# Weight conversions queued behind the last norm's scaling on VectorE and the last high part on ScalarE

## The chip, the cores and the metric

The kernel runs on one core of a Trainium2 chip. The metric is device time in microseconds (us), from one launch. Before the change three runs took 999.49, 1002.72 and 1003.02 us; the median is 1002.72. Profiles come from one more execution.

## The reference

Three stages, one behind the other, in float32 (weights are given as float64 and are read as pairs of 32-bit words):

```python
# attention: batch 4, heads 8, 512 local + 32 global positions, head size 64
s_ll = where(|i - j| <= 32, scale * q_l @ k_l.T, -1e9);  s_lg = scale * q_l @ k_g.T
out_l = softmax([s_lg, s_ll]) @ [v_g, v_l];  out_g = softmax(scale * q_g @ [k_g, k_l].T) @ [v_g, v_l]
x = concat([out_g, out_l]) as 2176 tokens x 512
# first feed-forward, 512 -> 1536 -> 512
xn = x / sqrt(mean(x * x) + 1e-6) * rms_g
x = (silu(xn @ w_gate) * (xn @ w_val)) @ w_out
# second feed-forward, 512 -> 2048 -> 512, with a rational function of h
h = x @ w_in;  g = P(h) / (Q(h) + 1e-6);  out = g @ w_out
```

## The kernel before

**Numbers in two parts.** Each matmul operand is split into a high part (rounded, `xt[:, 0]`, `ah`, `w[:, 0]`) and a low part (what the rounding left, `xt[:, 1]`, `al`, `w[:, 1]`); three products stand for one. On TensorE lines 644, 645 and 648 are the three for gate (psg) and value (psv), lines 676 to 678 the three for the way down (psA).

**Blocks, units, groups.** The 2176 tokens are eight blocks of 288 or 256 tokens (two per batch, the numbers in names: xt_4 belongs to block 4, psA_5_0 to block 5, quarter 0). The 1536 columns of the first feed-forward are three groups of four weight tiles. Group 0 runs over all eight blocks, then group 1, then group 2. One call of `unit()` is one step of a generator: a half of the gate and value products of one weight tile, or a quarter of the way down of the block before.

**Norm.** Before a block's first product its x is normed (`norm_stages`): ScalarE squares, VectorE or GpSimd adds, TensorE sums over partitions (psN, line 590), VectorE adds the epsilon (line 595), ScalarE takes an exponential as first guess of the root (line 598), VectorE improves it in two rounds of three small steps on 128x3 (lines 601 to 603, tile sm), TensorE spreads sm over partitions (psR, line 608), VectorE scales x in four instructions (line 614). Then `chunk` splits x: the high part on ScalarE (line 633, xt), the low part on VectorE or GpSimd (line 635). After a unit `act` makes a from psg and psv: ScalarE tanh (line 660), VectorE lines 662 and 663, ScalarE the high part ah (line 665), VectorE or GpSimd the low part al (line 667).

**Weight conversions.** `Weights.stages` turns one raw tile of float64 words into a high and a low part: ScalarE lines 89 and 92, VectorE lines 98, 100, 104 and 108 (tile cv), ScalarE line 118 (the high part), VectorE line 121 (the low part). `Weights.step` goes on with the tiles in work by one stage; the main loop calls it once per unit from unit 72 on (line 1039). Names raw_g, raw_v, raw_o, raw_h and raw_p are raw tiles of w_gate, w_val, w_out, w_in and the second w_out; w_g_4747 and w_v_4768 are the first two converted tiles of group 1.

**What sets the order.** Attention, all eight norms and the first 58 units are written out token by token in `SCRIPT`; inside `manual_schedule` every engine takes them in that order. What is traced behind it is placed by the framework's scheduler, which orders instructions by dependences, priority and its own estimate of time, and may put later traced instructions of an engine between those of the script. `tc.issue_after(ins)` adds an edge without a semaphore: whatever the block traces on the engine of `ins` is put behind `ins` in that engine's queue. Each engine runs its queue in order. With line 1002 the eight PSUM banks of attention are given back; the first tile of the new pools (psA of block 5) waits until all readers of the old banks are done, among them the scaling that reads the last psR.

Of the kernel before, what the change touches and what calls it, by code (L numbers as in the profile page):

```python
# [14 lines left out]
AF = mybir.ActivationFunctionType  # L15
# [19 lines left out]
def _ap(t, dims, offset=0):  # L35
    return bass.AP(tensor=t.tensor, offset=t.offset + offset, ap=[list(t.ap[0])] + [list(d) for d in dims])
# [496 lines left out]
class FFN1:  # L533
# [40 lines left out]
    def norm_stages(self, blk):  # L574

        nc = self.nc
        nb = self.width(blk)
        t = lambda i: self.pool.tile([128, NB1], F32, tag=f"st{i}", name=f"st{i}_{blk}", bufs=1)[:, :nb]
        m, r, u = t(0), t(1), t(2)
        nc.scalar.activation(out=m, in_=self.xs(blk, 0), func=AF.Square)  # L580
        yield
        for c, q in ((1, r), (2, u), (3, r)):
            nc.scalar.activation(out=q, in_=self.xs(blk, c), func=AF.Square)
            yield
            self.pick().tensor_tensor(out=m, in0=m, in1=q, op=ALU.add)
            yield c == 3
        cols = [min(128 * j, nb - 128) for j in range((nb + 127) // 128)]
        ps = self.bank(self.acc, f"psN{blk}")
        for j, c0 in enumerate(cols):
            nc.tensor.matmul(ps[:, j : j + 1], m[:, c0 : c0 + 128], self.ones, start=True, stop=True)  # L590
        yield
        n = len(cols)
        sm = self.pool.tile([128, 3, 3], F32, tag="sm", name=f"sm{blk}", bufs=2)
        m, r, u = (sm[:, i, :n] for i in range(3))
        nc.vector.tensor_scalar(out=m, in0=ps[:, :n], scalar1=1e-6, scalar2=None, op0=ALU.add)
        yield
        r0 = ps[:, 4 : 4 + n]
        nc.scalar.activation(out=r0, in_=m.bitcast(I32), func=AF.Exp, scale=-self.LN2H / 2**23, bias=self.eps)
        yield 1
        for up, to in ((1.0 + 1.65e-4, r0), (1.0, r)):  # L600
            nc.vector.scalar_tensor_tensor(out=u, in0=r0, scalar=-0.5 * up, in1=m, op0=ALU.mult, op1=ALU.mult)
            nc.vector.tensor_tensor(out=u, in0=u, in1=r0, op=ALU.mult)
            nc.vector.scalar_tensor_tensor(out=to, in0=u, scalar=1.5 * up, in1=r0, op0=ALU.add, op1=ALU.mult)
            yield
        ps = self.bank(self.acc, f"psR{blk}")
        for j, c0 in enumerate(cols):
            a = 128 * j - c0
            nc.tensor.matmul(
                ps[:, 128 * j : c0 + 128], _ap(r[:, j : j + 1], [[0, 128]]), self.ident[:, a:128], start=True, stop=True
            )  # L610
        yield
        for c in range(4):
            v = self.xs(blk, c)
            nc.vector.scalar_tensor_tensor(  # L614
                out=v, in0=v, scalar=self.gam[:, c : c + 1], in1=ps[:, :nb], op0=ALU.mult, op1=ALU.mult
            )
            yield
# [32 lines left out]
    def act(self, k, blk, pss, use_silu):  # L650
        nc = self.nc
        nb = self.width(blk)
        t = lambda tag, dt, bufs: self.pool.tile([128, NB1], dt, tag=tag, name=f"{tag}{blk}_{k}", bufs=bufs)[:, :nb]
        a, ah, al = t("a", F32, 2), t("ah", F32R, 6), t("al", F32R, 5)
        self.acts[blk, k] = ah, al
        g, v = pss[0][:, :nb], pss[1][:, :nb]
        if use_silu:
            self.last_silu = nc.scalar.activation(out=a, in_=g, func=AF.Silu)
        else:
            nc.scalar.activation(out=a, in_=g, func=AF.Tanh, scale=0.5)  # L660
            yield
            nc.vector.scalar_tensor_tensor(out=a, in0=a, scalar=1.0, in1=g, op0=ALU.add, op1=ALU.mult)
        nc.vector.scalar_tensor_tensor(out=a, in0=a, scalar=1.0 if use_silu else 0.5, in1=v, op0=ALU.mult, op1=ALU.mult)
        yield
        nc.scalar.activation(out=ah, in_=a, func=AF.Copy)
        yield
        self.pick().tensor_tensor(out=al, in0=a, in1=ah.bitcast(F32), op=ALU.subtract)

# [53 lines left out]
def ffn2(tc, pool, pp, y_all, coef, wts, out, side, opool):  # L722
# [19 lines left out]
    for bi, (s0, n) in enumerate(BLK2):  # L742
        yt = split_y(bi)
        ntt = n // 128
        acc = [pp.tile([128, 512], F32, tag="psB", name=f"psB{bi}_{m}", bufs=4) for m in range(ntt)]
        act, mid = {}, {}

        def up(k):
# [105 lines left out]
def kernel(  # L854
# [7 lines left out]
    nc = tc.nc  # L862
# [5 lines left out]
    wts = Weights(tc, vpool, wide)  # L868
# [12 lines left out]
    def cols(w, k):  # L881
        return w[:, 128 * k : 128 * k + 128].rearrange("(c p) f -> p c f", p=128)

    def rows(w, k):
        return w[128 * k : 128 * k + 128].rearrange("(c p) f -> p c f", p=128)

    def group_loads(grp, pool):
        for kk in range(4):
            k = 4 * grp + kk
            yield lambda k=k, kk=kk: wts.load(("g", k), pool, f"w{2 * kk}", cols(w_gate, k))  # L890
            yield lambda k=k, kk=kk: wts.load(("v", k), pool, f"w{2 * kk + 1}", cols(w_val, k))
        for kk in range(4):
            k = 4 * grp + kk
            yield lambda k=k, kk=kk: wts.load(("o", k), pool, f"w{8 + kk}", rows(w_out1, k))
# [3 lines left out]
    def load_2(k):  # L898
        (ph, th), (po, to) = slots2[2 * k], slots2[2 * k + 1]
        wts.load(("h", k), ph, th, cols(w_in2, k))  # L900
        wts.load(("p", k), po, to, rows(w_out2, k))

    NB = 2 * B
# [5 lines left out]
    def norm_step():  # L909
        if norms and not wts.on(norms[0]):  # L910
            norms.pop(0)

    def unit():
        done[0] += 1
        next(units, None)
# [12 lines left out]
    ffn = FFN1(tc, f1pool, x, y, gam, wts, ident)  # L928
# [69 lines left out]
        assert next(rest, 0) == 0  # L998
    att.eng = ffn.eng = wts.eng = None
    assert done[0] == IN_ATTN  # L1000
    manual.close()
    ps_scope.close()
    attn_scope.close()
# [15 lines left out]
    for n in range(IN_ATTN, 36 * NB):  # L1019
        blk, u = divmod(n, 12)  # L1020
        norm_step()
        if n == 12 * NB:
            silu[0] = True
        if blk == NB + 1 and u == 0:
            for f in group_loads(2, wa):
                f()
            for i in range(12):
                k = 10 + i // 2
                key, src = (("h", k), cols(w_in2, k)) if i % 2 == 0 else (("p", k), rows(w_out2, k))
                scratch[key] = (wa, f"w{i}", dram.tile([128, 2, 512], I32, name=f"scr{i}"))  # L1030
                wts.load(key, spare, f"s{i % 3}", src, scratch[key][2], True)
        if blk == 2 * NB + 1 and u == 0:
            for k in range(6):
                load_2(k)
        if blk > 2 * NB and blk % 2 == 0 and u == 6:
            load_2(6 + (blk - 2 * NB) // 2 - 1)
        unit()
        if n >= 72:
            wts.step(nc.vector, 2 if blk < NB + 1 else 1)
    for u in range(4):  # L1040
        unit()
    ps_scope.close()
# [50 lines left out]
```

## Time and profile before

| | |
|---|---|
| median of three runs | 1002.72 us |
| the profiled execution | 999.14 us |
| its span, first to last instruction | 997.4 us |
| TensorE busy | 944.8 us, 95% |
| VectorE busy | 784.7 us, 79% |
| ScalarE busy | 601.8 us, 60% |
| GpSimd busy | 311.5 us, 31% |
| mean granted TensorE clock | 0.980 of full speed |

The span is cut into three parts: attention with the first units up to about 250 us, the rest of the first feed-forward up to about 600 us, the second feed-forward behind it. In rows of a timeline the first number is the start, the second the length in us; "x4" are four instructions merged to one row; the bracket at the end gives how long the engine had been idle and whose end released it. Engines are PE (TensorE), DVE (VectorE), ACT (ScalarE), POOL (GpSimd), SP (SyncE).

### The profile page before, as it was taken

Reading aid. Unit: us, or ns where it says so; the run is one execution under the profiler, and the core shown is the slowest. Engines: PE = TensorE matmul, PEld = TensorE weight load, DVE = VectorE, ACT = ScalarE, POOL = GpSimd, SP = SyncE. Lnnn points to the kernel's source line nnn. Section 1 sums busy time; section 2 is a strip of 40 time slices with the busy share of each in tenths; the row PEclk is TensorE's granted clock in tenths of the full one; section 3 lists DMA queues with packets and bytes.
Section 4 is the critical chain, followed back from the end, with each engine's and each line's share of the span. In section 5 each row is a group of like instructions: output and inputs, shape, how many; then the busy total and the mean of one; then the engine's idle time right before and its main releaser. Section 6 shows DMA issues by size and latency. Waiting matters only on the chain.

```text
span 997.4 us, 21577 instructions
## 1 busy us (share of the span) xinstructions
PE 944.8 (95%) x8224; PEld 868.6 (87%) x8224; DVE 784.7 (79%) x1891; ACT 601.8 (60%) x1382; POOL 311.5 (31%) x406
## 2 busy tenths in 40 slices
PE   6677999997999999999999998999999999999997
PEld 4465898876999999999999997979899898898895
DVE  5787678768979987459954538998989989989897
ACT  6667657877658546337543335666667666666674
POOL 5444966632000000000000023543444435435443
PEclk9788999999899999999999999999999999999999
DMA  8887754327124055025011053000000000000000
GB/s 202 202 184 152 153 107 96 94 66 276 51 85 170 22 200 202 22 86 190 23 43 43 2 182 114 1 1 32 1 2 32 1 33 1 1 32 1 1 32 23
DMA packets 107576, 78.79 MB, mean 79 GB/s; under 512 B 72320, under 2 KB 95696, under 8 KB 107472
## 3 DMA queue, kind: packets, MB, share of 16 engines
q1 hardware_dynamic: 100672, 62.36, 22.2%
q0 software_dynamic: 5712, 14.79, 5.2%
q8 instruction: 65, 1.06, 0.5%
q10 hardware_dynamic: 1088, 0.26, 0.1%
q14 instruction: 39, 0.32, 0.1%
HBM read 62.64 MB, written 10.75 MB: 74 GB/s over the span
## 4 chain that ended last, share of the span: by engine, by line
PE 65%; DVE 16%; DMA 7%; ACT 4%; SPq 4%; issue 2%; POOL 2%; ACTq 0%; POOLq 0%; DVEq 0%
PE psg L644 4%; PE psA L676 4%; PE psA L678 4%; PE psA L677 4%; PE psv L644 4%; PE psg L648 4%; PE psg L645 4%; PE psv L648 4%; PE psv L645 4%; PE psH L755 4%; PE psH L756 4%; PE psH L757 4%; PE psB L790 4%; PE psB L791 4%; PE psB L792 4%; SPq L232 3%
## 5 line engine op out<-in xcount | busy, mean ns | idle before, releaser
L755 PE MATMUL psH<-yt,w_h 128*128 128x384 f32 (+1 forms) x384 | 126.0, 329 | 1.2 <-ACT yt L737 0.7
L756 PE MATMUL psH<-yt,w_h 128*128 128x384 f32 (+1 forms) x384 | 125.4, 327 | 0.0
L163 POOL TENSOR_SCALAR gh<-p 128x384 fp32r<-128x384 f32 (+1 forms) x96 | 59.0, 615 | 210.4 <-DVE p L779 181.6
L757 PE MATMUL psH<-yt,w_h 128*128 128x384 f32 (+1 forms) x384 | 123.5, 328 | 0.8 <-DVE yt L738 0.8
L644 PE MATMUL psg<-xt,w_g 128*128 128x288 f32 (+1 forms) x384 | 115.3, 302 | 0.7 <-ACT xt L633 0.6
L676 PE MATMUL psA<-ah,w_o 128*128 128x288 f32 (+1 forms) x384 | 111.8, 294 | 3.1 <-DVE x L614 2.0
L790 PE MATMUL psB<-w_p,gh 128*128 128x512 f32 x272 | 107.8, 396 | 5.1 <-POOL gh L163 5.1
L644 PE MATMUL psv<-xt,w_v 128*128 128x288 f32 (+1 forms) x384 | 111.3, 291 | 0.0
L645 PE MATMUL psg<-xt,w_g 128*128 128x288 f32 (+1 forms) x384 | 111.1, 290 | 0.0
L645 PE MATMUL psv<-xt,w_v 128*128 128x288 f32 (+1 forms) x384 | 110.9, 290 | 0.0
L678 PE MATMUL psA<-al,w_o 128*128 128x288 f32 (+1 forms) x384 | 110.0, 290 | 0.0
L677 PE MATMUL psA<-ah,w_o 128*128 128x288 f32 (+1 forms) x384 | 110.0, 290 | 0.0
L781 POOL TENSOR_TENSOR gl<-p,gh 128x384 fp32r<-128x384 f32 (+1 forms) x96 | 106.7, 1112 | 8.4 <-PE psB L792 0.4
L791 PE MATMUL psB<-w_p,gh 128*128 128x512 f32 x272 | 107.2, 394 | 0.0
L648 PE MATMUL psg<-xt,w_g 128*128 128x288 f32 (+1 forms) x384 | 105.3, 291 | 0.7 <-DVE xt L635 0.5
L648 PE MATMUL psv<-xt,w_v 128*128 128x288 f32 (+1 forms) x384 | 104.9, 290 | 0.0
L94 POOL TENSOR_SCALAR raw_h<-raw_h 128x512 int32<-128x512 uint32 x1 | 0.6, 644 | 332.5 <-DMA raw_h<-in_moe_w_in_dram 332.5
L775 ACT ACTIVATE r<-q,cq 128x384 f32<-128x384 f32 (+1 forms) x96 | 57.3, 597 | 60.4 <-DVE q L765 59.6
L765 DVE SCALAR_TENSOR_TENSOR q<-q,bv,t 128x384 f32<-128x384 f32 (+1 forms) x96 | 68.5, 713 | 21.9 <-ACT q L763 21.7
L792 PE MATMUL psB<-w_p,gl 128*128 128x512 f32 x272 | 82.0, 394 | 0.0
L764 ACT ACTIVATE p<-psH,av 128x384 f32<-128x384 f32 (+1 forms) x96 | 62.7, 653 | 27.7 <-POOL gl L781 27.4
L755 PEld LDWEIGHTS psH<-yt,w_h 128*128 128x128 f32 x384 | 72.2, 188 | 5.3 <-DVE p L767 1.5
(188 smaller groups left out, 2689.1 us busy)
## 6 DMA issues: line engine op xcount, KB each, us to landing
raw_h<-in_moe_w_in_dram SPq DMA_DIRECT2D x16, 512.0 KB, 3.9
raw_p<-in_moe_w_out_dram SPq DMA_DIRECT2D x16, 512.0 KB, 4.6
raw_g<-in_moe_w_gate_dram SPq DMA_DIRECT2D x12, 512.0 KB, 4.6
raw_v<-in_moe_w_val_dram SPq DMA_DIRECT2D x12, 512.0 KB, 5.3
raw_o<-in_moe_w_out_dram SPq DMA_DIRECT2D x12, 512.0 KB, 5.6
out_dram<-o SPq DMA_DIRECT2D x17, 256.0 KB, 2.0
x<-in_q_l_dram SPq DMA_DIRECT2D x48, 64.0 KB, 3.4
scr<-w_h SPq DMA_DIRECT2D x6, 512.0 KB, 3.5
```

Of the source, the lines that this page charges most:

```text
L644: nc.tensor.matmul(ps[j], part(j, 0, c), xt[c][:, 0], start=(c == 0), stop=False)
L645: nc.tensor.matmul(ps[j], part(j, 1, c), xt[c][:, 0], start=False, stop=False)
L648: nc.tensor.matmul(ps[j], part(j, 0, c), xt[c][:, 1], start=False, stop=(c == 3))
L676: nc.tensor.matmul(ps, wh, ah, start=(i == 0), stop=False)
L677: nc.tensor.matmul(ps, wl, ah, start=False, stop=False)
L678: nc.tensor.matmul(ps, wh, al, start=False, stop=(i == 3))
L755: nc.tensor.matmul(ph[:, :n], wh, yt[:, c, 0, :n], start=(c == 0), stop=False)
L756: nc.tensor.matmul(ph[:, :n], wl, yt[:, c, 0, :n], start=False, stop=False)
L757: nc.tensor.matmul(ph[:, :n], wh, yt[:, c, 1, :n], start=False, stop=(c == 3))
L790: nc.tensor.matmul(acc[m], gh[:, sl], wh, start=(k == 0), stop=False)
L791: nc.tensor.matmul(acc[m], gh[:, sl], wl, start=False, stop=False)
L792: nc.tensor.matmul(acc[m], gl[:, sl], wh, start=False, stop=(k == NC2 - 1))
```

## The change

The kernel keeps the last scaling instruction that the script traced on VectorE (line 614) and the last round to a high part on ScalarE (line 665). In the main loop the step of the conversions is traced inside `issue_after` of both: what it puts on VectorE goes behind the one, what it puts on ScalarE behind the other.

```diff
@@ norm_stages
-            nc.vector.scalar_tensor_tensor(
+            self.last_norm = nc.vector.scalar_tensor_tensor(
@@ act
-        nc.scalar.activation(out=ah, in_=a, func=AF.Copy)
+        self.last_high = nc.scalar.activation(out=ah, in_=a, func=AF.Copy)
@@ tile_attn_ffn_kernel
     assert done[0] == IN_ATTN
+    last_norm, last_high = ffn.last_norm.ins, ffn.last_high.ins
     manual.close()
...
         if n >= 72:
-            wts.step(nc.vector, 2 if blk < NB + 1 else 1)
+            with tc.issue_after(last_norm), tc.issue_after(last_high):
+                wts.step(nc.vector, 2 if blk < NB + 1 else 1)
```

VectorE's queue before, in the last norm of the script (psN_4325, sm_4356): small steps, and between them the two conversions.

```order
L601 SCALAR_TENSOR_TENSOR sm_4356<-psN_4325,sm_4356 128x3
L108 ISA cv_4692<-raw_g_4411,cv_4692 128x1024
L104 SCALAR_TENSOR_TENSOR cv_4712<-raw_v_4413,cv_4712 128x512
L602 TENSOR_TENSOR sm_4356<-sm_4356,psN_4325 128x3
L108 ISA cv_4712<-raw_v_4413,cv_4712 128x1024
L603 SCALAR_TENSOR_TENSOR psN_4325<-sm_4356,psN_4325 128x3
L667 TENSOR_TENSOR al_2_4277<-a_2_4275,ah_2_4276 128x256
L121 TENSOR_TENSOR w_g_4747<-cv_4692,w_g_4747 128x512
L601 SCALAR_TENSOR_TENSOR sm_4356<-psN_4325,sm_4356 128x3
L602 TENSOR_TENSOR sm_4356<-sm_4356,psN_4325 128x3
L121 TENSOR_TENSOR w_v_4768<-cv_4712,w_v_4768 128x512
L603 SCALAR_TENSOR_TENSOR sm_4356<-sm_4356,psN_4325 128x3
```

VectorE's queue now, from the same norm's second round of small steps to behind its scaling (x_0_76 and x_1_77 are its block's x, psR_4382 the spread sm).

```order
L667 TENSOR_TENSOR al_2_4277<-a_2_4275,ah_2_4276 128x256
L601 SCALAR_TENSOR_TENSOR sm_4356<-psN_4325,sm_4356 128x3
L602 TENSOR_TENSOR sm_4356<-sm_4356,psN_4325 128x3
L603 SCALAR_TENSOR_TENSOR sm_4356<-sm_4356,psN_4325 128x3
L667 TENSOR_TENSOR al_3_4352<-a_3_4350,ah_3_4351 128x256
L662 SCALAR_TENSOR_TENSOR a_0_4386<-a_0_4386,psg_0_4336 128x288
L663 SCALAR_TENSOR_TENSOR a_0_4386<-a_0_4386,psv_0_4337 128x288
L614 SCALAR_TENSOR_TENSOR x_0_76<-x_0_76,gam,psR_4382 128x288 x2
L614 SCALAR_TENSOR_TENSOR x_1_77<-x_1_77,gam,psR_4382 128x288 x2
L98 TENSOR_SCALAR cv_4692<-cv_4692 128x512
L100 TENSOR_SCALAR cv_4692<-cv_4692 128x512
L98 TENSOR_SCALAR cv_4712<-cv_4712 128x512
```

The conversions' steps have left the norm; between the second round of small steps and the scaling only lines 667, 662 and 663 are left, and the first conversion begins behind the scaling.

ScalarE's queue now, from the last high part of the script (ah_0_4387) on: ten conversion instructions, and then the eviction of psA of block 5, quarter 0, to y.

```order
L665 ACTIVATE ah_0_4387<-a_0_4386 128x288
L89 ACTIVATE cv_4692<-raw_g_4411 128x512
L92 ACTIVATE raw_g_4411<-raw_g_4411 128x512
L89 ACTIVATE cv_4712<-raw_v_4413 128x512
L92 ACTIVATE raw_v_4413<-raw_v_4413 128x512
L92 ACTIVATE raw_g_4415<-raw_g_4415 128x512
L92 ACTIVATE raw_v_4417<-raw_v_4417 128x512
L92 ACTIVATE raw_g_4419<-raw_g_4419 128x512
L92 ACTIVATE raw_v_4421<-raw_v_4421 128x512
L92 ACTIVATE raw_g_4423<-raw_g_4423 128x512
L92 ACTIVATE raw_v_4425<-raw_v_4425 128x512
L155 ACTIVATE y_4404<-psA_5_0_4440 128x256
```

Before, these ten stood among the norm's and the units' instructions, the first of them in front of the high parts xt_4; now they stand together.

## Rows read from the trace of the kernel before

**Rows 1.** Busy time by stretches; columns: stretch, length, busy time of each engine, clock, DMA.
```profile
220.00:260.00 40.00, 30.46 (x310) 29.04 (x310) 31.75 (x85) 27.74 (x60) 6.98 (x9) 0.87 0.57 205
260.00:340.00 80.00, 80.00 (x636) 80.00 (x635) 70.70 (x159) 53.55 (x119) 0.00 (x0) 1.00 0.24 80
340.00:400.00 60.00, 58.36 (x460) 57.54 (x459) 49.63 (x112) 32.38 (x72) 0.00 (x0) 1.00 0.51 176
```
**Rows 2.** TensorE's waits in the whole span: us in total, times, longest.
```profile
PE psR L608 <- DVE sm L603: 10.1, 2, 5.5
```
**Rows 3.** Timeline of TensorE around the last norm: start, length, instruction.
```profile
236.60 0.40 PE L644 MATMUL psg<-xt,w_g 128*128 128x288 f32 x1
...
240.47 0.29 PE L648 MATMUL psv<-xt,w_v 128*128 128x288 f32 x1
246.21 1.46 PE L608 MATMUL psR<-ident,sm 128*128 128x128 f32 x6 [5.45 <-DVE sm L603]
249.64 0.55 PE L676 MATMUL psA<-ah,w_o 128*128 128x256 f32 x1 [1.97 <-DVE x L614]
...
256.67 0.28 PE L676 MATMUL psA<-ah,w_o 128*128 128x256 f32 x1
```
**Rows 4.** Timeline of VectorE around the last norm.
```profile
235.42 0.42 DVE L98 TENSOR_SCALAR cv<-cv 128x512 f32<-128x512 f32 x1
...
236.96 1.65 DVE L614 SCALAR_TENSOR_TENSOR x<-x,gam,psR 128x256 f32<-128x256 f32 x4
...
240.38 0.15 DVE L595 TENSOR_SCALAR sm<-psN 128x3 f32<-128x3 f32 x1
...
245.91 0.15 DVE L603 SCALAR_TENSOR_TENSOR sm<-sm,psN 128x3 f32<-128x3 f32 x1
...
247.01 0.45 DVE L663 SCALAR_TENSOR_TENSOR a<-a,psv 128x288 f32<-128x288 f32 x1
247.71 1.79 DVE L614 SCALAR_TENSOR_TENSOR x<-x,gam,psR 128x288 f32<-128x288 f32 x4 [0.25 <-PE psR L608]
```
**Rows 5.** Timeline of VectorE in an earlier norm: first and last of six small steps.
```profile
229.68 0.16 DVE L601 SCALAR_TENSOR_TENSOR sm<-psN,sm 128x3 f32<-128x3 f32 x1
...
230.66 0.16 DVE L603 SCALAR_TENSOR_TENSOR sm<-sm,psN 128x3 f32<-128x3 f32 x1
```
**Rows 6.** Timeline of ScalarE around the last norm.
```profile
234.67 0.67 ACT L89 ACTIVATE cv<-raw_g 128x512 f32<-128x512 f32 x1 [1.71 <-DMA raw_g<-in_moe_w_gate_dram]
...
237.91 0.77 ACT L633 ACTIVATE xt<-x 128x288 fp32r<-128x288 f32 x2
...
245.74 0.65 ACT L92 ACTIVATE raw_v<-raw_v 128x512 int32<-128x512 uint32 x1
```
**Rows 7.** Timeline of TensorE: three starts behind a gap.
```profile
60.08 1.34 PE L421 MATMUL psT<-ident,p 128*128 128x128 f32 x4 [1.53 <-ACT p L416]
...
70.50 1.26 PE L503 MATMUL psOg<-vn,ptg 128*32 128x64 f32 x36 [2.89 <-DMA vn<-in_v_l_dram]
...
224.18 0.66 PE L432 MATMUL psO<-vw,pt 128*32 128x65 f32 x32 [1.82 <-ACT vw L155]
```
**Rows 8.** Busy time by stretches of 2 us; the clock is the third number from the end.
```profile
224.00:226.00 2.00, 1.82 (x41) 1.73 (x42) 0.83 (x3) 1.57 (x7) 0.80 (x1) 1.00 0.46 137
...
60.00:62.00 2.00, 1.92 (x8) 1.56 (x9) 2.00 (x6) 2.00 (x7) 1.09 (x1) 0.58 0.95 215
...
70.00:72.00 2.00, 1.50 (x38) 1.31 (x38) 1.90 (x9) 0.20 (x1) 0.39 (x2) 0.64 1.13 161
72.00:74.00 2.00, 2.00 (x37) 1.51 (x36) 1.33 (x5) 1.19 (x4) 1.84 (x4) 0.50 0.90 247
...
244.00:246.00 2.00, 0.00 (x0) 0.00 (x0) 1.97 (x9) 1.98 (x5) 0.00 (x0) 0.66 1.04 422
...
254.00:256.00 2.00, 2.00 (x13) 2.00 (x13) 1.65 (x4) 2.00 (x5) 0.00 (x0) 0.78 0.00 0
```
**Rows 9.** ScalarE's waits from 340 to 402 us: us in total, times, longest.
```profile
ACT cv L89 <- DMA raw_p<-in_moe_w_out_dram: 13.8, 5, 4.3
```

## The prediction

> **What bounds the kernel now.** I read the table by stretches first. From 260 to 340 us TensorE is busy for all 80 us, 636 matmuls, so 0.126 us each; from 220 to 260 it works only 30.46 of 40 us, at a mean clock of 0.87 [rows 1]. Behind a full stretch nothing can hide: what shortens the earlier one shortens the run, unless it is given back.
>
> The list of TensorE's waits names the cause: the broadcast matmul psR of a norm (line 608) waited twice for sm from VectorE (line 603), 10.1 us in all, the longest 5.5 us [rows 2]. The longest is in this stretch. On TensorE's timeline the last matmul of the unit before starts at 240.47 us, psR at 246.21, and behind psR comes a second wait of 1.97 us, until the scaling (line 614) has read psR's bank and psA may start at 249.64 [rows 3].
>
> VectorE's timeline shows why sm is late. psN, from which the norm goes on, was multiplied before 236.60 [rows 3], yet line 595 starts only at 240.38, and the last of the six small steps behind it ends at 246.06, 5.7 us later [rows 4]. In an earlier norm, with no conversions between, the same six took from 229.68 to 230.82 [rows 5]. The conversions of two weight tiles (w_g_4747 and w_v_4768, among the order's rows) stand between them in VectorE's queue, for weights of the next group. ScalarE has such work too: it idled 1.71 us for the load of raw_g, with the round of ah and four rounds of xt queued behind, and the last two of xt start only at 237.91 [rows 6].
>
> **What the change does there.** It adds and removes no instruction. On VectorE the ten instructions of two conversions and the first of a third go behind the last scaling; on ScalarE all conversions go behind the last round of ah. GpSimd keeps its order, and SyncE its own up to 244 us, so the loads start as before. TensorE's order stays the same up to the end of this block (psg_3, psv_3) and is shuffled a little after it.
>
> Step by step, in the times of the trace of before:
> - TensorE. 24 matmuls from 236.60 at 0.126 us, and the 0.3 us length of the last, end at 239.9 instead of 240.76: the short gaps between go, since the rounds of xt no longer stand behind conversions. psR could start at 239.9.
> - VectorE up to sm. Between line 98 at 235.42 and the four scalings of the norm before at 236.96 [rows 4] only a low part of xt of 0.4 us is left, so these start at 235.8 and end 1.6 us later at 237.4. Line 595 has its psN by then. Lines 662 and 663 of a_3 cost 0.85, the first three small steps 0.6, a low part of al 0.35 and the last three 0.55 [rows 4, 5]: sm is there at 239.75. psR started 0.15 us after sm before, so at 239.9 now: the wait of 5.45 us goes wholly.
> - psR to psA. psR took 1.46 us at half clock [rows 3], so 0.75 at full: 240.65. What is late next is VectorE: in front of the scaling it has lines 662 and 663 of a_0, which wait for ScalarE's tanh of psg_0 (complete at 239.9, then 0.4 us). At 0.45 us each, a little less net [rows 4], they run from 240.4 to 241.2; the four scalings take 1.79 us: 243.0. psA starts 0.14 us later, at 243.15 instead of 249.64. **First term: 6.5 us.** TensorE still idles 2.5 us.
> - The clock. Before, it fell from the higher level (2.4 GHz) to the lower (1.2 GHz): the two stretches with 0.66 and 0.78 place this between 244.6 and 254.9 us [rows 8]. The 36 matmuls from psA at 249.64 to the next psA at 256.67 took 7.03 us [rows 3]; at 0.126 us they take 4.53. **Second term: 2.5 us**, if the clock stays up.
>
> That is 9.0 us.
>
> **The unknown cost: the clock after 2.5 us of idleness.** Its ends are nothing and one fall. After a gap of 1.82 us the clock stayed at 1.00; after gaps of 1.53 and 2.89 us it was down, the second time for 1.44 us of one stretch of 2 us and all of the next: 3.4 us, which cost 1.7 us of matmul time [rows 7, 8]. Those two followed the small matmuls of attention and other gaps; the gap of 1.82 lies near dense matmuls, as ours does. And at this very place TensorE had been idle since 240.76 while the clock held until 244.6, 3.9 us [rows 3, 8]. That row is the nearest, so I take nothing and keep 1.7 for the range.
>
> A rule of the Trainium skill prices the clock otherwise. By "TensorE: Matmul & The Clock Gate", Terms, its cost is the time spent at the lower level times the share of pulses cut. For 10.3 us at half that would be 5.1 us, and the whole gain 10.9, a time near 988 us. The rows disagree: TensorE was idle in much of that time, and what the clock cost was 2.5 us there and 0.7 in psR, which the first term holds already. The sum goes by the rows.
>
> **What hides the moved conversions.** On ScalarE ten conversions of up to 0.67 us [rows 6] now stand between the last round of ah (241.2 to 241.65) and the eviction of psA's first bank, so this comes by 248.3. TensorE wants that bank for the fourth psA, 60 matmuls behind 243.15, at 250.7: a cover of 2.4 us. The last load that those ten read was there at 245.74 without a wait [rows 6]. VectorE then idles some 2 us for ScalarE's rounds in front of line 121, and line 662 of a_1 comes at about 251.5; its bank is wanted by psv_3, 98 matmuls behind 243.15, at 255.5: a cover of 4 us. If either failed, its lateness would go straight onto TensorE. Further on VectorE was busy 70.70 of the 80 us after 260 [rows 1]: 9.3 us are free for the eleven instructions that come later. I price all of this at nothing, from -1.6 (what TensorE lost between 340 and 400 us [rows 1], if a new alignment avoids it) to +5.
>
> **Rivals.**
> - A: the clock falls in the 2.5 us that are left. For it: the gap of 1.53 us. Gain 9.0 - 1.7 = 7.3: 991.8 us. The Trainium skill speaks for it too ("TensorE: Matmul & The Clock Gate", A second HAM failure mode): short idle spells between groups of matmuls, if frequent, make the clock swing. This trace bears that out only among the small matmuls of attention.
> - B: the backlog is paid later. ScalarE and VectorE run one or two conversions further behind the matmuls than before, and TensorE waits for a, ah or xt some time between 250 and 300 us. For it: covers of 2 to 4 us are not wide. Gain 3 to 5: 994 to 996.
> - C, the slower side: between 340 and 402 us ScalarE stands five times in line 89 for the load of raw_p, 13.8 us in all, the longest 4.3 [rows 9]. Rounds of xt or ah queued behind one of these make TensorE wait; before, they cost it 1.6 us together. The change shifts which rounds stand there. If four of them held up xt in full, some 3 us each, 12 us would be lost and the run 3 us slower: 1002. It decides from the third such hit, where the gain is used up. Against it: these loads are paced by work that comes earlier together with TensorE.
> - D: the edges don't act where the wait is, since al_3 or a_0 hold the scaling as long as the conversions did. Against it: only al and a stand there in the new order, fed by instructions that end before 241.3. Gain up to 2: 997 to 999.
>
> **How the numbers follow.** The profiled execution took 999.14 us, 1.74 over its span; the three timed runs lie 0.35, 3.58 and 3.88 above it, so their median 3.58. The forecast is 999.14 - 9.0 = 990.1 for an execution like the profiled one and 993.7 for one like the median; I give 992, between them, since I can't say which kind comes. Forecast 0.50 (its own range 989 to 994.5), A 0.25, B 0.15, C 0.05, D 0.05. The range 987.5 to 998 takes in A, B and the spread of the runs. A measurement of this kernel can tell about 0.5%, 5 us, from no change: the forecast, A and a little of B are faster by more, 0.78; most of B and D lie within, 0.17; C is slower, 0.05.
>
> **What would show it.** In the trace after: line 595 at about 237.4 and the last line 603 before 240; psR with no wait of over 1 us; psA's first matmul near 243, behind a wait for x (line 614) of about 2.5 us that replaces both; a clock of 1.00 from 240 to 260; no new wait of TensorE above 1 us between 250 and 300. A clock of 0.5 for some 3 us behind 243 is A; new waits for ah, a, y or xt are B or C; psR still at 244 or later is D, and I would be wrong at the first step.

## The result and the profile after

The changed kernel takes 988.47 us, median of 4 runs (987.83 to 988.81), beside 1001.86 us for the kernel before (999.49 to 1003.02; a fourth run, of 1000.99, has joined the three above). The ratio is 0.988, with a 95% interval of 0.9861 to 0.9898: faster by 1.0 to 1.4%. The forecast was 992, its range 987.5 to 998. The profiled execution took 988.8 us, its span 987.0, against 999.14 and 997.4 before.

The table by stretches, with the columns of [rows 1]:
```profile
220.00:260.00 40.00, 35.77 (x406) 34.75 (x405) 29.59 (x83) 28.72 (x68) 7.07 (x9) 1.00 0.59 210
260.00:340.00 80.00, 80.00 (x640) 80.00 (x640) 74.36 (x168) 53.81 (x118) 0.00 (x0) 1.00 0.23 80
340.00:400.00 60.00, 59.97 (x477) 59.70 (x476) 51.68 (x116) 33.30 (x72) 0.00 (x0) 1.00 0.51 176
```
From 220 to 260 us TensorE works 5.3 us more, and the clock is at its higher level throughout. The stretch behind it is as full as before, with VectorE 3.7 us busier: that is the backlog of conversions, and nobody waits for it. From 340 to 400 the 1.6 us that TensorE lost are gone too. ScalarE's waits for raw_p, 13.8 us in [rows 9], are down to 4.6 in the same part of the program, 330 to 393 us:
```profile
ACT cv L89 <- DMA raw_p<-in_moe_w_out_dram: 4.6, 2, 2.6
```
Part of the difference has only moved: a further wait of 1.92 us for raw_p ends at 393.69, just behind that part, and line 92 now waits 2.3 us for raw_h and raw_p.
Of the two waits for sm that [rows 2] adds up, only the earlier one is left:
```profile
PE psR L608 <- DVE sm L603: 4.7, 1, 4.7
```
TensorE around the last norm, to be laid beside [rows 3]. In this execution the block begins 1.21 us later (237.81 for 236.60), so 1.21 is to be taken off:
```profile
237.81 0.38 PE L644 MATMUL psg<-xt,w_g 128*128 128x288 f32 x1
...
240.95 0.29 PE L648 MATMUL psv<-xt,w_v 128*128 128x288 f32 x1
241.08 0.83 PE L608 MATMUL psR<-ident,sm 128*128 128x128 f32 x6
244.50 0.36 PE L676 MATMUL psA<-ah,w_o 128*128 128x256 f32 x1 [2.59 <-ACT raw_g L92]
...
249.19 0.28 PE L676 MATMUL psA<-ah,w_o 128*128 128x256 f32 x1
```
psR follows without a wait. One wait of 2.59 us stands in front of psA. The releaser in the bracket is the latest event that the profile could match, a conversion on ScalarE that psA doesn't read; what psA waits for is the last scaling, the fourth of the row L614 below, which ends at 244.35.

VectorE, beside [rows 4]:
```profile
238.74 0.15 DVE L595 TENSOR_SCALAR sm<-psN 128x3 f32<-128x3 f32 x1
...
240.77 0.16 DVE L603 SCALAR_TENSOR_TENSOR sm<-sm,psN 128x3 f32<-128x3 f32 x1
...
242.20 0.46 DVE L663 SCALAR_TENSOR_TENSOR a<-a,psv 128x288 f32<-128x288 f32 x1
242.57 1.78 DVE L614 SCALAR_TENSOR_TENSOR x<-x,gam,psR 128x288 f32<-128x288 f32 x4
```
From line 595 to the end of sm it is now 2.19 us instead of 5.68: only a_3 (lines 662 and 663) and one low part stand between.

ScalarE, beside [rows 6]: the ten conversions now stand together between the last round of ah and the eviction of psA's first bank.
```profile
242.69 0.44 ACT L665 ACTIVATE ah<-a 128x288 fp32r<-128x288 f32 x1 [1.08 <-DVE a L663]
243.16 0.67 ACT L89 ACTIVATE cv<-raw_g 128x512 f32<-128x512 f32 x1
...
248.24 0.66 ACT L92 ACTIVATE raw_v<-raw_v 128x512 int32<-128x512 uint32 x1
248.80 0.37 ACT L155 ACTIVATE y<-psA 128x256 f32<-128x256 f32 x1
```
The clock in the wait and behind it (stretch, length, TensorE's busy time, clock, DMA), where [rows 8] had 0.66:
```profile
242.00:244.00 2.00, 0.00 (x0) 1.00 1.09 380
244.00:246.00 2.00, 1.50 (x13) 1.00 1.08 418
```

Where the time came from is read off TensorE's timeline, divided at four marks that every kernel has: the first L644 of block 4, psA's first matmul, the second psA, and the second feed-forward's first matmul (L755). All lengths in us:
```
                 start  to psA  to 2nd psA  to L755  to end    span
before          236.60   13.04        7.03   347.21  393.52   997.4
after           237.81    6.69        4.69   344.71  393.10   987.0
difference       +1.21   -6.35       -2.34    -2.50   -0.42   -10.4
```
The norm gave 8.7 us, the stretch from the second psA to the second feed-forward another 2.5, the last stretch 0.4, and the start took 1.2 back. The same division is used for every experiment below.

### The profile page after: what moved, and what is told of

It reads as the page before. It is cut to its first block, busy times and chain, and to the rows that moved or that the text cites. A ratio compares the mean times of both kernels' runs of the same rounds, so it can differ in the third digit from the quotient of the medians.

```text
span 987.0 us, 21569 instructions
## 1 busy us (share of the span) xinstructions
PE 942.4 (95%) x8224; PEld 867.7 (88%) x8224; DVE 782.5 (79%) x1891; ACT 600.6 (61%) x1382; POOL 308.0 (31%) x406
## 4 chain that ended last, share of the span: by engine, by line
PE 77%; DVE 10%; DMA 5%; SPq 3%; ACT 3%; issue 1%; POOL 1%; ACTq 0%; POOLq 0%; DVEq 0%
PE psg L644 5%; PE psH L757 5%; PE psH L755 5%; PE psH L756 5%; PE psA L676 5%; PE psB L790 5%; PE psB L791 5%; PE psA L678 5%; PE psA L677 5%; PE psB L792 5%; PE psv L644 5%; PE psv L648 5%; PE psg L648 5%; PE psg L645 5%; PE psv L645 5%; SPq L232 3%
## 5 line engine op out<-in xcount | busy, mean ns | idle before, releaser
L755 PE MATMUL psH<-yt,w_h 128*128 128x384 f32 (+1 forms) x384 | 126.0, 329 | 1.2 <-ACT yt L737 0.7
L644 PE MATMUL psg<-xt,w_g 128*128 128x288 f32 (+1 forms) x384 | 115.0, 301 | 0.0
L644 PE MATMUL psv<-xt,w_v 128*128 128x288 f32 (+1 forms) x384 | 111.1, 290 | 0.0
L765 DVE SCALAR_TENSOR_TENSOR q<-q,bv,t 128x384 f32<-128x384 f32 (+1 forms) x96 | 71.2, 742 | 22.3 <-ACT q L763 22.2
L755 PEld LDWEIGHTS psH<-yt,w_h 128*128 128x128 f32 x384 | 72.2, 188 | 5.3 <-DVE p L767 1.5
```

The lines of the kernel that those rows point to most:

```text
L644: nc.tensor.matmul(ps[j], part(j, 0, c), xt[c][:, 0], start=(c == 0), stop=False)
L755: nc.tensor.matmul(ph[:, :n], wh, yt[:, c, 0, :n], start=(c == 0), stop=False)
```

## Experiments

Theory: VectorE's conversions held sm (first term), the idleness that followed lowered the clock (second term), and the later stretch gave 2.5 us because ScalarE's waits for raw_p and raw_h now fall elsewhere. Rivals: both edges are needed; the clock is a matter of its own; the bank that psA waits for is the larger cost; the later gain is chance. Each timed kernel ran beside the kernel before on the same chip (medians there 1000.74, 1001.12 and 1001.96 for the three groups of runs).

**One edge alone: VectorE.** Run e_dve.
```diff
-            with tc.issue_after(last_norm), tc.issue_after(last_high):
+            with tc.issue_after(last_norm):
```


> The changed kernel with the edge to the last scaling alone: the conversions leave VectorE until block 6's scalings are done, as in the changed kernel, but ScalarE keeps its rounds (L89, L92) between the high parts as before. My theory: VectorE held psR, so TensorE's wait for sm falls from 5.45 us to at most 1.5 (ScalarE's Exp, L598, now stands behind one L92 at 0.57 us, and six steps of 0.2 us follow), the wait in front of psA is 2.0 to 3.0, the clock stays at 1.00, and the time is 0.5 to 1.5 us above the changed kernel's 988.5. Rival: the two edges are needed together, since ScalarE's rounds hold Exp and a_0; then the wait for sm stays above 3 us, the clock falls, and the time is 4 to 7 us above the changed kernel's.

Measured: 996.51 us, ratio 0.9938 (0.9908 to 0.9969), so 4.2 us of gain. TensorE's timeline:
```profile
242.98 0.82 PE L608 MATMUL psR<-ident,sm 128*128 128x128 f32 x6 [1.02 <-DVE sm L603]
247.26 0.55 PE L676 MATMUL psA<-ah,w_o 128*128 128x256 f32 x1 [3.46 <-DVE x L614]
```
The wait for sm fell to 1.02 us, as the theory had it. The wait in front of psA did not stay within 3.0: it is 3.46, and the clock fell behind it (0.50 from 247 to 253). ScalarE's timeline shows what I had not counted:
```profile
242.03 0.66 ACT L92 ACTIVATE raw_v<-raw_v 128x512 int32<-128x512 uint32 x1 [0.58 <-DMA raw_v<-in_moe_w_val_dram]
...
243.42 0.65 ACT L92 ACTIVATE raw_g<-raw_g 128x512 int32<-128x512 uint32 x1 [0.43 <-DMA raw_g<-in_moe_w_gate_dram]
243.98 0.39 ACT L660 ACTIVATE a<-psg 128x288 f32<-128x288 f32 x1
```
The rounds of L92 don't only take 0.57 us each, they stand waiting for their own loads, and a_0 (line 660), which the scalings are queued behind on VectorE, stands behind them. The later stretch took 348.60 us, 1.4 more than before: TensorE waits 2.04 us there for xt, behind a wait of ScalarE for raw_h, and the clock falls once more (0.50 from 397 to 399). So the VectorE edge takes away the wait that [rows 2] names, and yet only 3.5 of the 8.7 us at the norm. The time is 8.0 us above the changed kernel's 988.5, more than either expectation had.

**One edge alone: ScalarE.** Run e_act.
```diff
-            with tc.issue_after(last_norm), tc.issue_after(last_high):
+            with tc.issue_after(last_high):
```


> The changed kernel with the edge to the last high part (ScalarE) alone. The order of instructions comes out the same as the changed kernel's on TensorE, VectorE and ScalarE, since each conversion begins on ScalarE and VectorE's share can't start before. My theory: the same time as the changed kernel, 987 to 990, with 11.4 us from block 4's first L644 to the second psA, 344.7 us from there to the second feed-forward, and TensorE without a wait between 340 and 400 us; what the median then moves against the kernel before is 11 to 13 us, of which the norm's stretch holds 8.7 and the later stretch 2.5. Rival: the changed kernel's times lay close together by luck, and on this chip they spread over 4 us and more like those of the kernel before; then its median is 990 or above.

Measured: 992.25 us (991.52 to 994.29), ratio 0.9905 (0.9878 to 0.9931). The traces show the changed kernel's order on all five engines, so this is a second look at it, and it shows the edge to the last scaling to be without effect: each conversion starts on ScalarE (L89), and what is held there is held on VectorE. The later stretch took 344.37 us with no wait of TensorE, as expected. But the clock fell this time. The wait, and the stretches behind it:
```profile
243.99 0.36 PE L676 MATMUL psA<-ah,w_o 128*128 128x256 f32 x1 [2.60 <-ACT raw_g L92]
```
```profile
244.00:245.00 1.00, 1.00 (x8) 0.89 1.09 430
246.00:247.00 1.00, 1.00 (x6) 0.50 1.04 426
```
From psA to the second psA it took 6.21 us instead of 4.69. With 2.0 us more in the last stretch, whose cause I did not follow, the gain on this chip was 8.9 us, not 11 to 13: the rival's median, 990 or above, came, though not its spread (2.8 us here).

**The changed kernel again.** Run e_again, with no edit.

> The changed kernel itself, unaltered, to see what it does from one execution to the next. My theory: behind the 2.6 us wait in front of psA the clock is sometimes lowered and sometimes not (the same order of instructions showed both), so the stretch from block 4's first L644 to the second psA is 11.4 or 12.9 us; the later stretch is a matter of order and stays at 344.4 to 344.7; the start (up to that L644) differs by some us; median 988 to 993. Rival: the lower clock came with the other kernel alone; then 11.4 again, and a median of 988.5.

Measured: 989.90 us (987.27 to 993.68), ratio 0.9877 (0.985 to 0.9904). TensorE's timeline, at the norm and later:
```profile
241.09 0.36 PE L676 MATMUL psA<-ah,w_o 128*128 128x256 f32 x1 [2.60 <-ACT raw_g L92]
...
389.67 0.40 PE L644 MATMUL psg<-xt,w_g 128*128 128x288 f32 x1 [0.70 <-ACT xt L633]
```
Again a wait of 2.60 us, and again the clock fell (0.50 from 243 to 245; 6.19 us to the second psA). So of three executions of one order, it fell in two. The later stretch took 345.92, which neither theory had: xt was 0.70 us late, behind a round of ScalarE that waited 1.83 us for raw_h. The order, the same on all engines, doesn't settle that stretch alone; in this execution when a load arrived had a share.

**TensorE kept busy in the wait.** Run e_fill.
```diff
         ps = self.bank(self.acc, f"psR{blk}")
+        if blk == 6:
+            for _ in range(22):
+                nc.tensor.matmul(ps[:, 0:128], self.ident, self.ident, start=True, stop=True)
```


> The kernel before with 22 spare matmuls of ident by ident into psR's own bank, in front of psR of block 6, each overwritten by psR: about 22 x 0.213 = 4.7 us of TensorE work in the wait of 5.45 us; everything else stands in the same order up to psA. My theory of the second term: the wait alone lowered the clock, so with TensorE busy the granted clock stays at 1.00, the 36 matmuls behind psA take 4.5 instead of 7.0 us, psA itself still begins where L614 lets it (13.2 us behind the first L644), and the time is 2.5 us below the kernel before. Rival: the clock falls anyway, or what it costs is taken up by a later wait; then no change.

Measured: 1000.07 us, ratio 0.9984 (0.9959 to 1.0009), no difference that can be told. From the first L644 to the second psA 18.90 us instead of 20.07. TensorE's timeline and the clock behind it:
```profile
245.39 5.07 PE L608 MATMUL psR<-ident 128*128 128x128 f32 x44
250.90 0.85 PE L611 MATMUL psR<-ident,sm 128*128 128x128 f32 x6 [0.43 <-DVE sm L603]
254.09 0.36 PE L679 MATMUL psA<-ah,w_o 128*128 128x256 f32 x1 [2.33 <-DVE x L617]
```
```profile
253.00:254.00 1.00, 0.00 (x0) 1.00 1.02 376
254.00:255.00 1.00, 0.91 (x5) 0.69 1.12 421
256.00:257.00 1.00, 1.00 (x6) 0.50 1.06 385
```
The spare matmuls held the clock through the long wait (psR took 0.85 instead of 1.46 us), but then it fell behind a wait of 2.33 us, shorter than the changed kernel's 2.59. In the stretch itself half of the expected 2.5 us came.

**A longer wait in the changed kernel.** Runs e_gap6 and e_gap3 (three copies instead of six).
```diff
+        if blk == 6:
+            for _ in range(6):
+                nc.vector.tensor_copy(out=junk, in_=ps[:, :nb])
         for c in range(4):
             v = self.xs(blk, c)
```


> The changed kernel with six spare copies of psR (128x288, about 0.43 us each) on VectorE ahead of block 6's scalings: TensorE's wait in front of psA grows from 2.59 to about 5.2 us. If a wait of that length lowers the clock, as the one of 5.45 us did before, the 36 matmuls behind psA take 7.0 instead of 4.5 us and the time rises by 2.6 + 2.5 = 5.1 us; if the clock stays at 1.00, by 2.6; if later waits have room, by less than either.

> The changed kernel with three spare copies of psR on VectorE ahead of block 6's scalings: TensorE's wait in front of psA grows from 2.59 to about 3.9 us. Waits of 2.33 us (with spare matmuls ahead) and of 5.41 us (six copies) were followed by the lower clock, the changed kernel's 2.59 us was not. If the clock stays at 1.00, 1.3 us more from the first L644 to the second psA; if it falls, 3.3 to 3.9 us more. Behind it: if the later stretch depends on how TensorE's blocks meet the chain of loads, it comes out between 344 and 351 us, whatever the wait; if it was the order of the conversions alone, at 344.7.

Measured: e_gap6 1001.41 us, ratio 0.9993 (0.997 to 1.0016); e_gap3 995.33, ratio 0.9933 (0.991 to 0.9957). The waits in front of psA were 5.41 and 3.94 us, the clock fell in both, and from the first L644 to the second psA it took 16.18 and 13.99 us. Up to there e_gap6 lost 4.8 us against the first execution of the changed kernel, as the higher expectation said; e_gap3 lost 2.6, less than the 3.3 expected with a fall. But the whole gain was gone, since the later stretch took 350.94 us, 6.2 more; in e_gap3 it took 347.08. The copies also shift the planned order on ScalarE, VectorE and, later, TensorE, so these two runs change more than the wait. One row of e_gap6's TensorE there:
```profile
385.12 0.40 PE L680 MATMUL psA<-ah,w_o 128*128 128x288 f32 x1 [2.76 <-ACT ah L669]
```
In that stretch ScalarE waited up to 5.7 us for raw_p, and ah came late behind it. TensorE's waits there add up to 4.2 us, and the clock fell behind the longest (0.50 from 386 to 388). This is rival C's mechanism, at half its price, with a fall of the clock in it that C had not counted.

**The stores out of the loads' way.** Run e_store, on the kernel before.
```diff
-            nc.sync.dma_start(out=scratch, in_=out.bitcast(I32))
+            nc.gpsimd.dma_start(out=scratch, in_=out.bitcast(I32))
```


> The kernel before with the twelve stores to scratch (L125) issued from POOL's queue instead of SP's, so that a load of raw_p or raw_h no longer stands behind a store there; the conversions behind attention stay as before. My theory of the 2.5 us that the later stretch gave: in the kernel before ScalarE stands in L89 for raw_p (13.8 us in all) just ahead of xt (L633), and TensorE waits three times for what comes behind (1.6 us); with earlier loads L89 waits under 6 us, the three waits go, and the stretch from the second psA to the second feed-forward falls from 347.2 to 344.7, the whole time by 2.5 us. Rival: the loads come no earlier (the transfers themselves are the limit), or the moved order puts another xt behind another wait; then the stretch stays above 346.5.

Measured: 1003.61 us, ratio 1.002 (1.0001 to 1.004). ScalarE's waits for raw_p and raw_h between 330 and 430 us fell from 16.4 to 9.1 us, the stretch from 347.21 to 346.53, no more: one wait for xt of 1.00 us took the place of three. My way of removing the cause fails; how much ScalarE waits matters less than what stands behind it then. The edit acts from 347 us on, so its norm is the kernel before once more, and there it took 21.54 us instead of 20.07. ScalarE's timeline shows why:
```profile
245.09 0.68 ACT L92 ACTIVATE raw_g<-raw_g 128x512 int32<-128x512 uint32 x1 [2.04 <-DMA raw_g<-in_moe_w_gate_dram]
245.66 0.40 ACT L665 ACTIVATE ah<-a 128x256 fp32r<-128x256 f32 x1
```
Behind ah ScalarE's line 118 comes late too, and VectorE stands for it in front of a conversion's last step (line 121), which the second round of small steps for sm is queued behind:
```profile
247.57 0.69 DVE L121 TENSOR_TENSOR w_g<-cv,w_g 128x512 fp32r<-128x512 f32 x1 [1.22 <-ACT w_g L118]
```
The old order makes sm wait for a load inside the norm, and by how much differs from one execution to the next.

**The bank in front of psA.** Runs e_banks and e_banks2 (the changed kernel, twice) and e_bb (the kernel before), all with this edit:
```diff
-    pp = ps_scope.enter_context(tc.tile_pool(name="ps2", bufs=1, space=PSUM))
+    pp = ps_scope.enter_context(tc.tile_pool(name="ps2", bufs=1, space=PSUM, reuse_waits="tile"))
```


> The changed kernel with the banks behind attention handed over one by one: psA no longer waits for VectorE's scaling (L614) of block 6, but for the high and low part of a_3 alone; the order on every engine is the same. My theory: the 2.59 us that TensorE still stands in front of psA go, psA starts with psR's end at about 242.0, the fourth psA finds its bank evicted with 0.3 us to spare, and the time falls by 2.6 us against the changed kernel, to 986. Rival: ScalarE's ten conversions now hold the evictions and the next high parts, so TensorE loses the 2.6 us again at a later wait; no change.

> The changed kernel with the banks behind attention handed over one by one, a second time, beside the changed kernel on the same chip. My theory: TensorE's longest wait there is 0.83 us, the clock is not lowered in any execution, and the time is 1.7 us (clock held in the changed kernel) to 3.2 us (clock lowered there) below the changed kernel's. Rival: what is gained at the norm is lost behind it; within 1 us of the changed kernel.

> The kernel before with the banks behind attention handed over one by one; the order on every engine is that of the kernel before. My theory: the wait of 5.45 us in front of psR stays, since VectorE still holds sm, the lower clock stays, and only the wait of 1.97 us in front of psA goes: 18.1 us from the first L644 to the second psA instead of 20.1, 2 us off the time. Rival: the moved conversions were not needed and the bank's wait was the larger cost; then 5 us or more off the time.

Measured: e_banks 988.34 us, ratio 0.9865 (0.9832 to 0.9898); e_banks2 986.80, ratio 0.9845 (0.9817 to 0.9873), 3.1 us below the changed kernel (e_again) on the same chip, with six runs of each that overlap (983.22 to 991.48 beside 987.27 to 993.68); e_bb 997.26, ratio 0.9953 (0.9932 to 0.9974). e_banks2 on TensorE:
```profile
237.47 0.82 PE L608 MATMUL psR<-ident,sm 128*128 128x128 f32 x6
238.12 0.37 PE L676 MATMUL psA<-ah,w_o 128*128 128x256 f32 x1
...
240.89 0.37 PE L644 MATMUL psv<-xt,w_v 128*128 128x288 f32 x1 [0.83 <-DVE x L614]
```
psA follows psR at once, and 0.83 us of the wait reappears in front of a matmul that, to judge by the scaling it waits for, was given psR's bank. From the first L644 to the second psA it takes 9.68 us in both, against 11.38 or 12.9, so that 1.7 of the 2.6 us expected came beside the first execution; the clock stayed at 1.00 in both. In e_bb the wait for sm stays:
```profile
246.88 1.46 PE L608 MATMUL psR<-ident,sm 128*128 128x128 f32 x6 [5.44 <-DVE sm L603]
248.16 0.56 PE L676 MATMUL psA<-ah,w_o 128*128 128x256 f32 x1
```
The stretch takes 16.72 us, 3.4 less than before: 2.1 for the wait, 1.2 because the clock rose sooner. That is more than the 2 us expected, and the medians moved by 4.7, close to the 5 us that the rival asked for. But the wait for sm and the fall of the clock stay, and the stretch is 5.3 us longer than the changed kernel's 11.38. So the bank is the smaller cost, and the moved conversions were needed.

**Both.** Run e_best: the changed kernel with the edits of e_banks and e_store.
```diff
+    pp = ps_scope.enter_context(tc.tile_pool(name="ps2", bufs=1, space=PSUM, reuse_waits="tile"))
...
+            nc.gpsimd.dma_start(out=scratch, in_=out.bitcast(I32))
```


> The changed kernel with both: banks handed over one by one, and the stores to scratch on POOL's queue. My theory: the later stretch has no wait left to lose, so the stores give nothing there (344.4 us, within 0.5), the banks give 1.7 us at the norm, and the time is 1.7 us below the changed kernel's on the same chip. Rival: with the order of the conversions moved, TensorE waits for an xt or a high part between 340 and 400 us again, and the time is 1 to 4 us above the changed kernel's.

Measured: 990.22 us, ratio 0.988 (0.9849 to 0.9912), 2.0 us below e_act on the same chip; 9.68 us at the norm, 344.32 behind it. The stores give nothing, as expected. The best version is the changed kernel with the banks handed over one by one; the stretch at the norm, 9.68 us in all three executions, shows it more firmly than the medians do.

All profiled executions, divided at the same marks:
```
           start  to psA  to 2nd psA  to L755  to end   span  waits before psA, clock behind them
before    236.60   13.04        7.03   347.21  393.52   997.4  5.45 + 1.97, fell
e_bb      237.25   10.91        5.81   347.38  394.45   995.8  5.44, fell
e_store   238.43   14.82        6.72   346.53  395.20  1001.7  7.24 + 1.98, fell
e_fill    241.38   12.71        6.19   347.17  393.55  1001.0  0.43 + 2.33, fell
e_dve     237.97    9.29        7.32   348.60  393.32   996.5  1.02 + 3.46, fell
e_gap6    238.44    9.50        6.68   350.94  393.64   999.2  5.41, fell
e_gap3    239.01    8.04        5.95   347.08  394.12   994.2  3.94, fell
after     237.81    6.69        4.69   344.71  393.10   987.0  2.59, held
e_act     237.30    6.69        6.21   344.37  395.13   989.7  2.60, fell
e_again   234.40    6.69        6.19   345.92  393.10   986.3  2.60, fell
e_banks   239.98    3.92        5.76   344.36  394.68   988.7  none (0.83 later), held
e_banks2  234.20    3.92        5.76   344.37  393.15   981.4  none (0.83 later), held
e_best    240.00    3.92        5.76   344.32  394.30   988.3  none (0.83 later), held
```

## Why the prediction was right, and where it was not

- The first term, 6.5 us, measured 6.35, and each of its steps came out: with 1.21 us taken off, sm is complete at 239.72 (239.75 forecast), psR starts at 239.87 (239.9), psA at 243.29 (243.15). All three executions of this order give 6.69 us from the first L644 to psA. What the prediction did not see is which edge does it: ScalarE's alone (e_act), and VectorE's alone leaves psA 2.6 us later (e_dve), because ScalarE waits for loads with a_0 behind it. [rows 6] showed such a wait, the 1.71 us for raw_g; I read it as a delay of xt alone, and counted only the short gaps that it left on TensorE.
- The second term, 2.5 us, measured 2.34 where the clock held. The other price that the prediction worked out for the clock, 5.1 us and a time near 988, lies nearer to the median by chance: the clock gave back 2.34 us behind psA and 0.63 in psR (0.83 us for 1.46).
- The clock. I took nothing for the 2.5 us of idleness and gave rival A, the fall, 0.25. It held in the execution that was profiled with the result, which was luck: it fell in two others of the same order. There the stretch from the first L644 to the second psA took 12.9 us, so the gain was 7.2; A's sum was 7.3, with 1.7 for the fall, which measured 1.5. The nearest row was the wrong ground: that the clock had held for 3.9 us of idleness once didn't say that it would hold for 2.5. The Trainium skill's "TensorE: Matmul & The Clock Gate", A second HAM failure mode, lays such a loss to idle spells that are short but frequent; here one single spell of 2.6 us sufficed, two times of three.
- The covers held: psA's first bank is evicted at 249.2 and wanted at 252.0, line 662 of a_1 starts at 251.97, and TensorE has no wait between 250 and 340. Rivals B and D are out.
- The step that failed is the price of nothing for what comes further on. The later stretch gave 2.5 us (2.8 and 1.3 in the other two executions), past the -1.6 that I had allowed as its best end. TensorE's three waits there, 1.64 us together, are gone. Counted from start to start they had cost 2.1, since the first matmul behind a wait is longer (0.40 for 0.29 us). The rest is in no row that I can name. Rival C had the right place, with the sign open: over the experiments this stretch took 344.3 to 350.9 us. e_store shows that fewer waits alone don't bring the gain, e_again that one order gives 344.4 to 345.9. That the order has a part is shown: the kernel before took 347.2 and 347.4 (e_bb), and the changed order, in five executions, 344.4 to 344.7 four times and 345.9 once. That the arrival of loads has one rests on that one execution, and which round of ScalarE must stand where is not shown.
- The base. Terms of 9.0 us were set against 999.14, and I put the forecast between the profiled execution and the median. In spans the gain was 10.4: 8.7, 2.5 and 0.4 in the last stretch, less 1.2 of a later start. The medians moved by 13.4, 8.9 (e_act) and 12.1 (e_again). Part of what lies beyond the sum is the kernel before, whose norm took 21.54 us in e_store's execution: its stretch depends on when loads arrive, and the profiled execution, faster than each of the four timed runs, was a good one of it. Where the rest lies is not shown: of the timed runs there is no trace, and in the traces the start and the last stretch each differ by some us.

## What to carry to other kernels

When an engine's queue mixes work on the critical path with work for later, look at what the later work waits for and not only at how long it runs: a conversion that stands waiting for its load holds all that is queued behind it. Hold back such a chain at its first engine; the engines behind it follow by themselves, and an edge there is idle, as e_act's order shows. When two waits stand one behind the other, a shortened one may leave just enough idleness for the clock to fall, so it pays to remove the second too (here a bank's handover, 1.7 to 3.2 us).

## What the runs showed of the hardware beyond that

- The same instructions behind the same wait of 2.6 us met a lowered clock in two executions and the full one in a third. 2.33 us lowered it in another kernel (e_fill), and so did 2.04 us in e_dve's later stretch; 2.09 us did not at 225 us of e_act, nor 0.83 us in three executions. Between 2.0 and 2.6 us the length of the wait alone does not tell. A fall at the norm cost 1.5 us here.
- The fall can come when TensorE is already at work again. In e_again psA starts at 241.09 us, the clock is 1.00 up to 242.5 and 0.50 behind it. In e_dve's later stretch the matmuls behind the wait start at full speed and then slow down:
```profile
395.70 0.40 PE L644 MATMUL psg<-xt,w_g 128*128 128x288 f32 x1 [2.04 <-ACT xt L633]
...
396.33 0.29 PE L644 MATMUL psg<-xt,w_g 128*128 128x288 f32 x1
...
396.89 0.45 PE L645 MATMUL psv<-xt,w_v 128*128 128x288 f32 x1
```
- The first L644 of block 4 starts anywhere from 234.2 to 241.4 us, though hardly an edit acts before it. e_banks and e_banks2 have the same instructions in the same order, and differ by 5.8 us there and by 7.3 in span; they ran on two chips, so that chip and chance are not told apart. The start is not the whole of the spread: the first execution of the changed kernel and e_act, again of one order, differ by 2.7 us in span, 1.5 from the clock and 2.0 from the last stretch, with the start 0.5 earlier.
